# Starting the second layer pair's weight preparation earlier, behind other work and with three places

## The chip, the cores and the metric

The kernel runs on one core of a Trainium2 chip. The metric is the device time of one launch in microseconds (us), the median of several runs. Engines are TensorE (PE in the profile; PEld is its weight load), VectorE (DVE), ScalarE (ACT), GpSimd (POOL) and SyncE (SP), which issues all DMA transfers here.

## The reference

```python
# attention: 4 x 8 heads, 768 positions, head size 64, chunks of 32 with 16 keys to the left, 8 to the right, 8 memory keys
out[:, :, c_start:c_end] = softmax(q_c @ k_full.T / sqrt(D)) @ v_full
x = attn_out as (3072 tokens, 512)
# first layer pair ("moe"): w_in 512 x 2048, w_out 2048 x 512
h = x @ w_in
x = (h * clip(h + 3, 0, 6) / 6) @ w_out
# second layer pair ("moe2"), same shapes
h = x @ w_in
return maximum(0.01 * h, h) @ w_out
```

## The kernel before, in words

All products are made of fp32 values that are split into two fp32r parts, a high one and a low one; three products (high by high, low by high, high by low) stand for one. The tokens are cut into six blocks of 512 (`N`). The first layer pair works on units: unit f of block j makes 128 columns of the hidden layer (`hidden`, L602: 12 matmuls at L615, then `gate` at L627 on ACT, `times` at L630 on DVE, and the split `two_parts`, a cast on ACT and a subtraction), and `output` (L642) multiplies them by 128 rows of the second weight into four PSUM banks (12 matmuls at L662). TensorE takes hidden of unit i, then output of unit i - 1. Blocks 0 and 1 (`TWICE` = 2) are done in halves: block 0 units 0 to 7, block 1 units 0 to 7, block 0 units 8 to 15, block 1 units 8 to 15. So their output sums leave the banks twice: the first halves go through the `ys` tiles to `half` in DRAM, and at the end of the second half `y_out` (L681) reads them back (L699), adds the bank (`plus`, L696) and stores the sum to `spill` (L703). The other blocks' sums are copied once (`take`, L689) and stored to `spill`.

The second layer pair takes blocks in pairs of 1024 tokens and uses seven products instead of eight on 2 x 2 blocks. Its operands of activations come from `x_pair` (L715, with `x_quarter`, L725): loads from `spill`, subtractions on DVE, and splits. Its weights are prepared once, in the course of the first pair, by `prepare` (L788), 16 times, for w_in (kept as `kepti`) and w_out (`kepto`) in turn. One preparation:

- two calls of `decode` (L327): each loads 512 KB (L332) into one of the 33 `w` tiles, 32 of which hold the first pair's weights, takes an absolute value on ACT (L335) into one of two `wm` tiles and does four operations on DVE (L338 to L350). The loads come `after=splits[-2:]`, the last two splits of the first pair's weights; `gate=chain` puts ACT's operation behind the preparation before.
- four sums and differences of quarters (`form`, L804; L805) in place in the `wm` tiles, and seven times `parts_of` (L807): a high part (cast on ACT) and a low part (DVE) into one of the four `ys` tiles, which `keep` (L782) stores to DRAM (L784). The `ys` tile is free again when the store has landed.

`left` (L827) loads the kept parts back later (L835).

The order of all instructions comes from a planner, `schedule` (L83). It runs the tasks through a model of the engines at build time: each engine has a heap of ready tasks, and takes the one with the lowest key. Keys are positions in TensorE's sequence of products, in which a unit of the first pair takes 6; `progress` counts how far TensorE has come. A task is put in a heap when what it depends on is done and its key is at most `progress + AHEAD` (60). A task that needs new tiles (`allocs`) waits until there is a place (`blocked`, L108). The engines then execute the planned order strictly, each its own queue, with semaphore waits. The first pair takes keys 0 to 576; the preparations have keys 200 + 21 k (`PREPARE`, `EVERY`), their loads 30 less; `x_pair` for the first pair of blocks has keys 510 and 528; a gate's key is its unit's position less 12.

Of the kernel before, what the change touches and what calls it, by code (L numbers as in the profile page):

```python
# [9 lines left out]
F32 = mybir.dt.float32  # L10
# [31 lines left out]
LEFT_OF = {1: "a11", 2: "a12", 3: "s4", 4: "a22", 5: "s1", 6: "s2", 7: "s3"}  # L42
ORDER = FIRST + THEN
RING, OPS = 6, 6
PREPARE, EVERY = 200, 21
T1_IN = ("wm", "wm", "st", "st", "r", "r")
RIGHT_OF = {1: "b11", 2: "b21", 3: "b22", 4: "t4", 5: "t1", 6: "t2", 7: "t3"}

# [2 lines left out]
class Task:  # L51


    def __init__(self, fn, opts, key, after=(), allocs=(), uses=(), moe=False, issues=1):
        self.fn, self.opts, self.key, self.moe, self.issues = fn, opts, key, moe, issues
        self.allocs, self.next, self.left, self.ready = allocs, [], 0, 0.0
        self.bufs = list(allocs) + list(uses)
        self.taken = False
        for b in self.bufs:
            b.users += 1  # L60
        for t in after:
            t.next.append(self)
            self.left += 1


class Buf:


    def __init__(self, tag):
        self.tag, self.users, self.t = tag, 0, None  # L70


QUEUED = 6000.0
# [3 lines left out]
OTHER = 20  # L77
# [5 lines left out]
def schedule(tasks, places):  # L83
# [15 lines left out]
    def offer(task):  # L99
        nonlocal n  # L100
        n += 1
        if task.key > progress + AHEAD:
            heapq.heappush(future, (task.key, n, task))
            return
        for i, e in enumerate(task.opts):
            heapq.heappush(heaps[e], (task.key + (OTHER if i else 0), n, task))

    def blocked(task):  # L108
        for b in task.allocs:
            if len(live[b.tag]) >= places[b.tag]:  # L110
                return b.tag
        return None

# [94 lines left out]
def tile_attn_moe_moe2(ctx: ExitStack, tc: tile.TileContext, raw, w1i, w1o, w2i, w2o, out):  # L208
# [115 lines left out]

    wbuf, wtask = {}, {}

    def decode(src, f, key, early=None, after=(), place="wm", gate=()):  # L327

        t, m = Buf("w"), Buf(place)

        def load(e):
            nc.sync.dma_start(out=make(t, ([128, 512, 2], U32)).rearrange("p w s -> p (w s)"), in_=src[f])  # L332

        def absolute(e):
            nc.scalar.activation(out=make(m, ([128, 512], F32)), in_=t.t[:, :, 1].bitcast(F32), func=AF.Abs)  # L335

        def clamp(e):
            engine(e).tensor_scalar(out=m.t, in0=m.t, scalar1=W_MOST, scalar2=W_LEAST, op0=ALU.min, op1=ALU.max)  # L338

# [12 lines left out]
        k = add(load, {"SP": dma(524288)}, key - 30 if early is None else early, after=after, allocs=[t])  # L352
        k = add(absolute, {"ACT": act(512)}, key, after=[k, *gate], allocs=[m], uses=[t])
        k = add(clamp, {"DVE": dve2(512)}, key + 0.1, after=[k], uses=[m])
        k = add(bits, {"DVE": dve2(512)}, key + 0.2, after=[k], uses=[m])
        k = add(sign, {"DVE": dve(512)}, key + 0.3, after=[k], uses=[m, t])
        k = add(low, {"DVE": dve(512)}, key + 0.4, after=[k], uses=[m, t])
        return m, k

    def split_w(which, f, m, k, key):  # L360
# [219 lines left out]
            to_x(jb + 1, t, pos_h["1", jb + 1, 0] - BLK + 4, 0, first, NU, src=st)  # L580


    gbuf, gtask, yend, ybuf, yhalf, firsts = {}, {}, {}, {}, {}, []
    last = [None]

    def product(fn, n, after, allocs=(), uses=(), count=4):
# [52 lines left out]
    def bank(b):  # L639
        return made(b)  # L640

    def output(lay, j, f, c0, n):  # L642
        t0 = blocks[j][0]

        halves = (KF // 2, KF) if j < TWICE else (KF,)
        begin = c0 == 0 and f in (0, *halves)
        end = f + 1 in halves
        if begin:
            ybuf[lay, j] = banks_of(False)
        banks = ybuf[lay, j]  # L650
        ys = banks
        g, w = gbuf[lay, j, f, c0], wbuf[lay + "o", f]
        ghi, glo = gtask[lay, j, f, c0]
        whi, wlo = wtask[lay + "o", f]
        order = [(d, p) for p in range(3) for d in range(KD)]
        if end:
            order.sort()

        def part(some):
            def fn(e):  # L660
                for d, p in some:
                    nc.tensor.matmul(  # L662
                        bank(banks[d])[:, c0:c0 + n], w.t[:, 1 if p == 1 else 0, d * 128:(d + 1) * 128], g.t[:, 1 if p == 2 else 0, :n],
                        start=(begin and p == 0), stop=(end and p == 2), skip_group_check=True,
                    )
            return fn

        ks = []
        for i in range(3):
            some = order[4 * i:4 * i + 4]  # L670
            need = [whi, wlo, ghi] if end or i else [whi, ghi]
            if end or i == 2:
                need.append(glo)

            ks.append(product(part(some), n, need, allocs=ys if begin and i == 0 else (), uses=[w, g] + ([] if begin and i == 0 else ys)))
        if end:
            yend[lay, j] = []
            for d in range(KD):
                y_out(lay, j, f, t0, N, d, banks[d], ks[(3 * d + 2) // 4], len(halves) > 1)

    def y_out(lay, j, f, t0, n, d, y, k, two):  # L681
        s = Buf("ys")
        key = pos_y[lay, j, f] - 12
        scale = 1.0 / 6.0
        dst = spill[d, :, t0:t0 + n]
        if two and f < KF - 1:
            dst = half[j, d]

        def take(e):  # L689
            if e == "ACT":  # L690
                nc.scalar.mul(make(s)[:, :n], bank(y)[:, :n], scale)
            else:
                nc.vector.tensor_scalar(out=make(s)[:, :n], in0=bank(y)[:, :n], scalar1=scale, scalar2=None, op0=ALU.mult)

        def plus(e):
            nc.vector.scalar_tensor_tensor(out=s.t, in0=bank(y), scalar=scale, in1=s.t, op0=ALU.mult, op1=ALU.add)  # L696

        if two and f == KF - 1:
            l = add(lambda e: nc.sync.dma_start(out=make(s), in_=half[j, d]), {"SP": dma(n * 512)}, key - 8, after=[yhalf[j, d], *firsts], allocs=[s])  # L699
            k = add(plus, {"DVE": dve(n)}, key, after=[k, l], uses=[s, y])  # L700
        else:
            k = add(take, {"DVE": dve(n)} if d % 2 and two else {"ACT": act(n, 50.0)}, key, after=[k], allocs=[s], uses=[y])
        k = add(lambda e: nc.sync.dma_start(out=dst, in_=s.t[:, :n]), {"SP": dma(n * 512)}, key, after=[k], uses=[s])  # L703
        yhalf[j, d] = k
        if two and f < KF - 1:
            firsts.append(k)
        yend[lay, j].append(k)
# [74 lines left out]
    def keep(which, slot, src, after, uses, key):  # L782
        def fn(e):
            nc.sync.dma_start(out=kept[which][slot // 2, :, slot % 2], in_=src().bitcast(F32))  # L784

        kdone[which, slot] = add(fn, {"SP": dma(262144, 330.0)}, key, after=after, uses=uses)

    def prepare(which, src, i, key):  # L788


        parts = [decode(src, 2 * i + c, key + 6 * c, after=splits[-2:], gate=chain) for c in range(2)]
        raws, l = [m for m, _ in parts], [k for _, k in parts]
        chain[:] = l
        key += 12
# [7 lines left out]
            return raws[c].t[:, o:o + 256]  # L802

        def form(out, x, y, op, after):  # L804
            return [add(lambda e: engine(e).tensor_tensor(out=part(out), in0=part(x), in1=part(y), op=op), {"DVE": dve(256)}, key, after=after, uses=raws)]  # L805

        def parts_of(n, after):  # L807
            t, b = Buf("ys"), raws[at[n][0]]
            hi = add(lambda e: copy(e, make(t, ([128, 2, 256], F32R))[:, 0], part(n)), {"ACT": act(256)}, key, after=after, allocs=[t], uses=[b])
            lo = add(lambda e: minus(e, t.t[:, 1], part(n), t.t[:, 0].bitcast(F32)), {"DVE": dve(256)}, key, after=[hi], uses=[b, t])  # L810
            q = [LEFT_OF[m] for m in ORDER].index(n)
            keep(which, 7 * i + q if which == "i" else KF // 2 * q + i, lambda: t.t, [hi, lo], [t], key + 2)
            return [hi, lo]
# [341 lines left out]
```

## Time and profile before

| | us |
|---|---|
| median of 3 runs (lowest, highest) | 1114.21 (1111.7, 1115.73) |
| the profiled execution | 1105.18 |
| its span, first to last instruction | 1103.4 |
| TensorE busy in the span | 1061.6 |
| VectorE busy | 707.5 |
| ScalarE busy | 532.0 |

Times in the trace are counted from the start of the span. "Busy" counts instructions in flight; matmuls overlap, so TensorE's busy time is not its peak. In a timeline, a row has the start, the time taken, the engine, the line, and the operation as output <- inputs with buffer numbers left out; in brackets stands the idle time before it and what released it. "SPq" is the queue of SyncE with the time that an issue took there.

### The profile page before, as it was taken

The page shows a single profiled execution, that of the slowest core. Times are in us where ns is not written, and L with a number is a line of the kernel's source. Part 1 is how long each engine was busy: PE and PEld are TensorE (multiplying, and loading weights), DVE is VectorE, ACT ScalarE, POOL GpSimd, SP SyncE. Part 2 cuts the span into 40 slices and gives each one's busy share as a digit, 9 for nine tenths or more (in the row PEclk, how much of TensorE's full clock was granted, in tenths as well). Part 3 has the DMA queues.
Part 4 walks back from the last instruction along what each step waited for, and adds up shares of the span by engine and source line. Part 5 has one row for each costly group of instructions (what it writes and reads, how often), then busy time and mean ns, then how long its engine had stood idle before and what let it go on. Part 6 is the DMA issues. An engine that isn't in the chain of part 4 may idle for free.

```text
span 1103.4 us, 19981 instructions
## 1 busy us (share of the span) xinstructions
PE 1061.6 (96%) x7488; PEld 872.8 (79%) x7488; DVE 707.5 (64%) x1230; ACT 532.0 (48%) x1297; POOL 114.2 (10%) x112
## 2 busy tenths in 40 slices
PE   4599999999999999999999899999999999999998
PEld 3487888888878788788887688888888888888887
DVE  4789982526666566466678435499466696366673
ACT  4657554525666555455455333375234464233532
POOL 1130000101223222212222200000000000000000
PEclk9999999999999999999999999999999999999999
DMA  8886414505566555365477346668765786766763
GB/s 198 246 221 203 172 65 113 156 22 182 173 179 199 159 175 191 124 188 170 139 239 254 106 143 224 236 219 323 256 220 211 266 294 248 249 221 226 260 217 115
DMA packets 105120, 215.22 MB, mean 195 GB/s; under 512 B 10816, under 2 KB 43584, under 8 KB 105024
## 3 DMA queue, kind: packets, MB, share of 16 engines
q1 hardware_dynamic: 105024, 213.95, 59.3%
q8 instruction: 59, 0.97, 0.4%
q14 instruction: 37, 0.30, 0.1%
HBM read 163.58 MB, written 50.33 MB: 194 GB/s over the span
## 4 chain that ended last, share of the span: by engine, by line
PE 77%; DVE 7%; DMA 7%; ACT 3%; SPq 2%; issue 2%; POOL 0%; ACTq 0%; DVEq 0%
PE y L662 17%; PE h L615 17%; PE y L997 12%; PE y L879 10%; PE h L997 6%; PE hx L879 6%; PE h L879 4%; PE hx L997 3%; DMA w<-in_raw 2%; DMA a<-in_raw 2%; DMA w<-in_w1o 2%; DVE ys L292 1%; PE at L493 1%; SPq L397 1%; DVE wm L346 1%
## 5 line engine op out<-in xcount | busy, mean ns | idle before, releaser
L662 PE MATMUL y<-g,w 128*128 128x512 f32 x1152 | 283.8, 393 | 8.1 <-ACT g L289 5.3
L662 PEld LDWEIGHTS y<-g,w 128*128 128x128 f32 x1152 | 216.2, 189 | 56.5 <-ACT g L289 6.6
L615 PE MATMUL h<-xh,w 128*128 128x512 f32 x768 | 196.3, 395 | 1.6 <-ACT xh L289 1.6
L615 PEld LDWEIGHTS h<-xh,w 128*128 128x128 f32 x768 | 143.7, 189 | 32.5 <-ACT xh L289 2.6
L630 DVE SCALAR_TENSOR_TENSOR r<-r,h 128x512 f32<-128x512 f32 x96 | 65.8, 685 | 106.8 <-ACT r L627 106.7
L292 POOL TENSOR_TENSOR g<-r,g 128x512 fp32r<-128x512 f32 x64 | 88.6, 1385 | 332.0 <-ACT g L289 315.3
L627 ACT ACTIVATE r<-h,three 128x512 f32<-128x512 f32 x96 | 66.5, 693 | 109.0 <-PE h L615 108.5
L292 DVE TENSOR_TENSOR w<-w 128x512 fp32r<-128x512 f32 (+1 forms) x162 | 105.5, 687 | 17.4 <-ACT w L289 16.5
L615 PE MATMUL h<-xl,w 128*128 128x512 f32 x384 | 104.1, 393 | 0.0
L854 ACT ACTIVATE w<-w 128x512 f32<-128x512 f32 x48 | 30.3, 632 | 132.1 <-DVE w L911 100.2
L997 PE MATMUL y<-w 128*128 128x512 f32 x384 | 90.0, 389 | 0.0
L289 ACT CAST g<-r 128x512 fp32r<-128x512 f32 x97 | 60.5, 624 | 58.2 <-DVE r L630 53.3
L615 PEld LDWEIGHTS h<-xl,w 128*128 128x128 f32 x384 | 72.3, 189 | 15.4
L997 PEld LDWEIGHTS y<-w 128*128 128x128 f32 x384 | 72.1, 188 | 15.0
L292 DVE TENSOR_TENSOR ys<-wm,ys 128x256 fp32r<-128x256 f32 x112 | 61.2, 568 | 20.4 <-ACT ys L289 20.2
L879 PE MATMUL y<-w 128*128 128x512 f32 x264 | 61.8, 389 | 0.0
L289 ACT CAST g<-w 128x512 fp32r<-128x512 f32 x50 | 31.0, 622 | 63.8 <-PE y L997 34.3
L289 ACT CAST w<-w 128x512 fp32r<-128x512 f32 x102 | 58.3, 618 | 6.2 <-DVE w L292 4.5
L879 PEld LDWEIGHTS y<-w 128*128 128x128 f32 x264 | 49.6, 188 | 10.3
L335 ACT ACTIVATE wm<-w 128x512 f32<-128x512 f32 x56 | 37.6, 673 | 33.3 <-DVE ys L292 9.2
L289 ACT CAST ys<-wm 128x256 fp32r<-128x256 f32 x112 | 41.8, 410 | 23.5 <-DVE wm L350 14.6
L292 DVE TENSOR_TENSOR g<-w,g 128x512 fp32r<-128x512 f32 x50 | 34.0, 689 | 28.7 <-ACT g L289 28.5
(160 smaller groups left out, 1515.8 us busy)
## 6 DMA issues: line engine op xcount, KB each, us to landing
w<-kepti SPq DMA_DIRECT2D x84, 512.0 KB
w<-kepto SPq DMA_DIRECT2D x84, 512.0 KB
kepti<-ys SPq DMA_DIRECT2D x56, 256.0 KB
kepto<-ys SPq DMA_DIRECT2D x56, 256.0 KB
a<-in_raw SPq DMA_DIRECT2D x44, 224.0 KB
w<-in_w1i SPq DMA_DIRECT2D x16, 512.0 KB
w<-in_w1o SPq DMA_DIRECT2D x16, 512.0 KB
w<-in_w2i SPq DMA_DIRECT2D x16, 512.0 KB
```

The costliest lines, as they stand in the source:

```text
L289: nc.scalar.copy(out, in_) if e == "ACT" else engine(e).tensor_copy(out=out, in_=in_)
L292: engine(e).tensor_tensor(out=out, in0=a, in1=b, op=ALU.subtract)
L335: nc.scalar.activation(out=make(m, ([128, 512], F32)), in_=t.t[:, :, 1].bitcast(F32), func=AF.Abs)
L346: nc.vector.scalar_tensor_tensor(out=mu, in0=t.t[:, :, 1], scalar=0xC0000000, in1=mu, op0=ALU.bitwise_and, op1=ALU.bitwise_or)
L397: nc.sync.dma_start(out=qk[i].t[r], in_=of_raw(par, r, slice(0, QK))[i].rearrange("g d c -> d g c"))
L615: nc.tensor.matmul(h.t[:, :n], w.t[:, 1 if p == 1 else 0, k * 128:(k + 1) * 128], x[:, k, c0:c0 + n], start=(p == 0 and k == 0), stop=(p = ...
L627: nc.scalar.activation(out=make(r)[:, :n], in_=h.t[:, :n], func=AF.Relu, bias=three[:, 0:1], scale=1.0)
L630: nc.vector.scalar_tensor_tensor(out=r.t[:, :n], in0=r.t[:, :n], scalar=6.0, in1=h.t[:, :n], op0=ALU.min, op1=ALU.mult)
L662: nc.tensor.matmul(bank(banks[d])[:, c0:c0 + n], w.t[:, 1 if p == 1 else 0, d * 128:(d + 1) * 128], g.t[:, 1 if p == 2 else 0, :n], start= ...
L854: return add(lambda e: nc.scalar.activation(out=at(), in_=at(), func=AF.Prelu, alpha=0.01), {"ACT": act(N)}, key, after=[after], uses=uses)
L879: nc.tensor.matmul(bank(to), t.t[:, o, l, kt * 128:(kt + 1) * 128].bitcast(F32R), operand(p, name, 1 if q == 2 else 0, kt).bitcast(F32R), ...
L997: nc.tensor.matmul(bank(to[d]), w.t[:, o, 1 if q == 1 else 0, d * 128:(d + 1) * 128].bitcast(F32R), g.t[:, 1 if q == 2 else 0], start=(fre ...
```

## The change

Preparation k has the key 112 + 22 k instead of 200 + 21 k. All its tasks but the loads get `late=60`: this is added to their key for the rank in an engine's heap, but not for the moment from which they may be taken. Its parts may take a `ys` tile only while that leaves at most three of the four in use (`Buf("ys", 3)`). A task that needs several tiles of a kind at once (the four banks of an output, or two) waits until there is room for all of them.

The reload of a half sum now begins with a one-column copy on ACT that takes the `ys` tile and waits for the last product of output unit f - 3 (`ylast`); the DMA follows it. The copies of the first half sums, of which two in four ran on DVE, run on ACT.

```diff
-PREPARE, EVERY = 200, 21
+PREPARE, EVERY, LATE = 112, 22, 60
...
 class Buf:
-    def __init__(self, tag):
-        self.tag, self.users, self.t = tag, 0, None
+    def __init__(self, tag, most=99):
+        self.tag, self.most, self.users, self.t = tag, most, 0, None
...
         for i, e in enumerate(task.opts):
-            heapq.heappush(heaps[e], (task.key + (OTHER if i else 0), n, task))
+            heapq.heappush(heaps[e], (task.key + task.late + (OTHER if i else 0), n, task))
...
     def blocked(task):
+        tags = [b.tag for b in task.allocs]
         for b in task.allocs:
-            if len(live[b.tag]) >= places[b.tag]:
+            if len(live[b.tag]) + tags.count(b.tag) > min(places[b.tag], b.most):
                 return b.tag
...
+        ylast[j, f] = ks[-1]
         if end:
...
         def take(e):
-            if e == "ACT":
-                nc.scalar.mul(make(s)[:, :n], bank(y)[:, :n], scale)
-            else:
-                nc.vector.tensor_scalar(out=make(s)[:, :n], in0=bank(y)[:, :n], scalar1=scale, scalar2=None, op0=ALU.mult)
+            nc.scalar.mul(make(s)[:, :n], bank(y)[:, :n], scale)
...
         if two and f == KF - 1:
-            l = add(lambda e: nc.sync.dma_start(out=make(s), in_=half[j, d]), {"SP": dma(n * 512)}, key - 8, after=[yhalf[j, d], *firsts], allocs=[s])
+            l = add(lambda e: nc.scalar.copy(make(s)[:, :1], three), {"ACT": act(1)}, key - 8, after=[yhalf[j, d], *firsts, ylast[j, f - 3]], allocs=[s])
+            l = add(lambda e: nc.sync.dma_start(out=s.t, in_=half[j, d]), {"SP": dma(n * 512)}, key - 8, after=[l], uses=[s])
             k = add(plus, {"DVE": dve(n)}, key, after=[k, l], uses=[s, y])
         else:
-            k = add(take, {"DVE": dve(n)} if d % 2 and two else {"ACT": act(n, 50.0)}, key, after=[k], allocs=[s], uses=[y])
+            k = add(take, {"ACT": act(n, 50.0)}, key, after=[k], allocs=[s], uses=[y])
...
-        kdone[which, slot] = add(fn, {"SP": dma(262144, 330.0)}, key, after=after, uses=uses)
+        kdone[which, slot] = add(fn, {"SP": dma(262144, 330.0)}, key, after=after, uses=uses, late=LATE)
...
-            t, b = Buf("ys"), raws[at[n][0]]
+            t, b = Buf("ys", 3), raws[at[n][0]]
```

The other lines pass `late=LATE` to the operations of `decode`, `form` and `parts_of`.

## Rows read from the trace of the kernel before

**Rows 1.** The page, part 1: busy us, share of the span, instructions.

```profile
PE 1061.6 (96%) x7488; PEld 872.8 (79%) x7488; DVE 707.5 (64%) x1230; ACT 532.0 (48%) x1297; POOL 114.2 (10%) x112
```

**Rows 2.** TensorE's waits: releaser, us in total, times, longest us.

```profile
PE y L662 <- ACT g L289: 5.3, 2, 4.6
...
PE y L662 <- ACT ys L691: 2.8, 2, 2.3
```

**Rows 3.** Windows by stage: stretch, length, busy (instructions) per engine, clock, DMA share, GB/s.

```profile
160.00:255.00 95.00, 95.00 (x873) 78.11 (x873) 37.48 (x65) 38.40 (x118) 4.38 (x4) 1.00 0.35 95
255.00:560.00 305.00, 301.05 (x2678) 246.09 (x2677) 193.11 (x349) 169.62 (x499) 73.59 (x54) 1.00 0.55 172
560.00:618.00 58.00, 52.65 (x223) 42.30 (x222) 50.25 (x90) 30.08 (x61) 14.25 (x10) 0.97 0.72 239
636.00:1103.00 467.00, 463.53 (x2046) 383.48 (x2044) 293.03 (x459) 193.13 (x334) 1.29 (x1) 1.00 0.66 232
```

**Rows 4.** Timeline from 605 to 618 us.

```profile
605.93 0.68 ACT L627 ACTIVATE r<-h,three 128x512 f32<-128x512 f32 x1
...
607.85 1.07 PE L615 MATMUL h<-xl,w 128*128 128x512 f32 x4
...
612.19 0.68 DVE L630 SCALAR_TENSOR_TENSOR r<-r,h 128x512 f32<-128x512 f32 x1
...
612.90 0.62 ACT L289 CAST g<-r 128x512 fp32r<-128x512 f32 x1 [2.15 <-DVE r L630]
...
613.57 4.50 PE L662 MATMUL y<-g,w 128*128 128x512 f32 x12 [4.65 <-ACT g L289]
```

**Rows 5.** The chain of work that ended last: start, us, twelve output matmuls.

```profile
626.25 2.72 PE y L662 x12
```

**Rows 6.** VectorE's groups from 560 to 620 us, of preparation: busy us, mean ns.

```profile
L292 DVE TENSOR_TENSOR ys<-wm,ys 128x256 fp32r<-128x256 f32 x26 | 16.0, 641 | 2.0 <-ACT ys L289 2.0
L805 DVE TENSOR_TENSOR wm<-wm 128x256 f32<-128x256 f32 x15 | 7.3, 490 | 0.1
```

**Rows 7.** Timeline of SyncE's queue: reloads, first load, spills, first and last stores.

```profile
168.12 1.77 SPq L699 DMA_DIRECT2D ys<-half  x4
169.93 0.43 SPq L332 DMA_DIRECT2D w<-in_w2i  x1
170.40 11.75 SPq L397 DMA_DIRECT2D a<-in_raw  x4
...
206.93 0.35 SPq L703 DMA_DIRECT2D spill<-ys  x1
...
257.15 1.32 SPq L703 DMA_DIRECT2D spill<-ys  x3
259.38 0.32 SPq L784 DMA_DIRECT2D kepti<-ys  x1
...
608.74 8.66 SPq L784 DMA_DIRECT2D kepto<-ys  x7
```

**Rows 8.** Timeline of ACT, one cycle of preparation, 505 to 527 us.

```profile
505.23 1.02 ACT L289 CAST ys<-wm 128x256 fp32r<-128x256 f32 x3 [2.68 <-DVE wm L350]
...
511.67 0.44 ACT L289 CAST ys<-wm 128x256 fp32r<-128x256 f32 x1
513.73 0.72 ACT L335 ACTIVATE wm<-w 128x512 f32<-128x512 f32 x1
...
523.41 0.67 ACT L335 ACTIVATE wm<-w 128x512 f32<-128x512 f32 x1 [0.35 <-DMA w<-in_w2o]
526.63 1.01 ACT L289 CAST ys<-wm 128x256 fp32r<-128x256 f32 x3
```

**Rows 9.** Timeline around 157 us: last split of the first pair's weights.

```profile
157.10 0.62 ACT L289 CAST w<-wm 128x512 fp32r<-128x512 f32 x1
```

**Rows 10.** ACT's prices: ns min/median/max of copies; group of accumulator reads, us, ns.

```profile
L691 ACT ACTIVATE ys<-y x20: 580/598/628, 112.2 to 648.1; 128x512 f32<-128x512 f32 x20
...
L462 ACT ACTIVATION_READ_ACCUMULATOR a<-at,mx 128x1 f32 x132 | 30.2, 229 | 0.0
```

More of the change, by code (lines that the diff above doesn't have):

```diff
@@ L51, with __init__ @@
 class Task:
-    def __init__(self, fn, opts, key, after=(), allocs=(), uses=(), moe=False, issues=1):
+    def __init__(self, fn, opts, key, after=(), allocs=(), uses=(), moe=False, issues=1, late=0):
+        self.late = late
         self.fn, self.opts, self.key, self.moe, self.issues = fn, opts, key, moe, issues
@@ L325, in tile_attn_moe_moe2, with decode @@
     wbuf, wtask = {}, {}
-    def decode(src, f, key, early=None, after=(), place="wm", gate=()):
+    def decode(src, f, key, early=None, after=(), place="wm", gate=(), late=0):
         t, m = Buf("w"), Buf(place)
@@ L352, in decode @@
         k = add(load, {"SP": dma(524288)}, key - 30 if early is None else early, after=after, allocs=[t])
[L353 to L357, printed above, removed]
+        k = add(absolute, {"ACT": act(512)}, key, after=[k, *gate], allocs=[m], uses=[t], late=late)
+        k = add(clamp, {"DVE": dve2(512)}, key + 0.1, after=[k], uses=[m], late=late)
+        k = add(bits, {"DVE": dve2(512)}, key + 0.2, after=[k], uses=[m], late=late)
+        k = add(sign, {"DVE": dve(512)}, key + 0.3, after=[k], uses=[m, t], late=late)
+        k = add(low, {"DVE": dve(512)}, key + 0.4, after=[k], uses=[m, t], late=late)
         return m, k
@@ L580, in unit @@
             to_x(jb + 1, t, pos_h["1", jb + 1, 0] - BLK + 4, 0, first, NU, src=st)
-    gbuf, gtask, yend, ybuf, yhalf, firsts = {}, {}, {}, {}, {}, []
+    gbuf, gtask, yend, ybuf, yhalf, ylast, firsts = {}, {}, {}, {}, {}, {}, []
     last = [None]
@@ L784, in fn @@
             nc.sync.dma_start(out=kept[which][slot // 2, :, slot % 2], in_=src().bitcast(F32))
-        kdone[which, slot] = add(fn, {"SP": dma(262144, 330.0)}, key, after=after, uses=uses)
+        kdone[which, slot] = add(fn, {"SP": dma(262144, 330.0)}, key, after=after, uses=uses, late=LATE)
     def prepare(which, src, i, key):
-        parts = [decode(src, 2 * i + c, key + 6 * c, after=splits[-2:], gate=chain) for c in range(2)]
+        parts = [decode(src, 2 * i + c, key + 6 * c, after=splits[-2:], gate=chain, late=LATE) for c in range(2)]
         raws, l = [m for m, _ in parts], [k for _, k in parts]
@@ L804, in form @@
         def form(out, x, y, op, after):
-            return [add(lambda e: engine(e).tensor_tensor(out=part(out), in0=part(x), in1=part(y), op=op), {"DVE": dve(256)}, key, after=after, uses=raws)]
+            return [add(lambda e: engine(e).tensor_tensor(out=part(out), in0=part(x), in1=part(y), op=op), {"DVE": dve(256)}, key, after=after, uses=raws, late=LATE)]
         def parts_of(n, after):
-            t, b = Buf("ys"), raws[at[n][0]]
-            hi = add(lambda e: copy(e, make(t, ([128, 2, 256], F32R))[:, 0], part(n)), {"ACT": act(256)}, key, after=after, allocs=[t], uses=[b])
-            lo = add(lambda e: minus(e, t.t[:, 1], part(n), t.t[:, 0].bitcast(F32)), {"DVE": dve(256)}, key, after=[hi], uses=[b, t])
+            t, b = Buf("ys", 3), raws[at[n][0]]
+            hi = add(lambda e: copy(e, make(t, ([128, 2, 256], F32R))[:, 0], part(n)), {"ACT": act(256)}, key, after=after, allocs=[t], uses=[b], late=LATE)
+            lo = add(lambda e: minus(e, t.t[:, 1], part(n), t.t[:, 0].bitcast(F32)), {"DVE": dve(256)}, key, after=[hi], uses=[b, t], late=LATE)
             q = [LEFT_OF[m] for m in ORDER].index(n)
```

## The prediction

> **What bounds the kernel now.** I began with the busy shares on the page: TensorE has an instruction in flight for 1061.6 of 1103.4 us, VectorE for 707.5 [rows 1]. So the question is where TensorE stands idle, 41.8 us in all, and which of that the change can reach. The windows by stage answer the first half: from 160 to 255 us it loses nothing, from 255 to 560 us 3.95, from 560 to 618 us 58.0 - 52.65 = 5.35 us, and from 636 us to the end 3.5 us of 467 [rows 3]. The remaining 29 us lie nearly all before 160 us, ahead of any preparation. The list of TensorE's waits then names two that stand in the middle of the span: 5.3 us for a gate's cast (ACT g), 4.6 us of it in one place, and 2.8 us for output copies (ACT ys) [rows 2].
>
> The timeline around 605 to 618 us shows the one large wait. A gate (L627) ends at 606.61, but VectorE comes to its product (L630) only at 612.19; the cast follows at 612.90 and the output matmuls at 613.57, while the last hidden matmul had ended at 608.92 [rows 4]. So TensorE stands for 4.65 us behind VectorE's queue. The twelve matmuls after it take 4.50 us, against 2.72 us for the same twelve soon afterwards [rows 4, 5]: another 1.78 us, and the granted clock of the stretch is 0.97 instead of 1.00 [rows 3], so some of them ran at the lower of its two levels, 1.2 GHz, after TensorE had stood. Earlier in the same tail there is a wait of 0.66 us of the same kind (the rest of the 5.3 us). The tail costs 5.3 + 1.8 = 7.1 us.
>
> What fills VectorE there? Of its 50.25 us in that stretch, the preparation's splits and forms alone (L292 on ys, L805) take 16.0 + 7.3 = 23.3 us [rows 3, 6], beside the bit work on the same weights and the first operands of the second pair. Preparation and x_pair fall on each other.
>
> **Why it is late.** The preparation is a chain, and not held up by keys. The row of stores shows its first store at 259.38 and its last seven from 608.74 [rows 7], 15 cycles of 23.3 us. One cycle reads as follows: first part cast at 505.23, the fifth at 511.67 (the first to get a place back, 6.4 us later), the next preparation's first half decoded from 513.73, its second half from 523.41, first part cast at 526.63 [rows 8]. It starts late because all four ys places are full: the reloads of block 0's half sums are issued at 168.12 though its spills leave only at 206.93, and block 1's hold the places until its spills at 257.15 [rows 7]. The first weight load was out at 169.93 [rows 7].
>
> **The change part by part.**
> *Start.* The key of 112 is not what decides: the loads still wait for the last two splits of the first pair, whose cast is at 157.10 [rows 9]. So the first load can go at about 158 instead of 169.93. What decides is that the reloads now wait for the output of unit f - 3. From the end of that unit to the next needed bank there are five groups of twelve matmuls and then the first bank's three: 5 x 2.72 + 0.68 = 14.3 us [rows 5]. The places are then held for some 20 us at each of the two block ends instead of from 168 to 257 us nearly without a break. Following a cycle by hand with the durations of rows 8: preparation 0 forms its parts from about 176, preparation 1 from about 212 (behind block 0's reloads), preparation 2 from 231 with a break at block 1's end, and preparation 3 begins decoding at about 259. Before, preparation 0 stood there: two preparations and some 7 us, 2 x 23.3 + 7 = 54 us of lead.
>
> *Cap of three.* Bounds: nothing, or one more turn of a place, 6.4 us a preparation [rows 8]. The next decode needs the raw half that the fourth and fifth parts use last. With four places the fifth part is the first of the second round; with three it is the second of that round, so it comes only a fraction of a microsecond later, and only the seventh part slips by a whole round, which the next half's load covers. I take 0.8 us, near the lower end: 13 x 0.8 = 10 us of the lead. Perfetto Trace Analysis in the Trainium skill, under "Identifying the Most-Contended Engine", says that gaps that repeat can mean that there are too few buffers; taking a place away would then lengthen every cycle by the upper bound. By that rule 13 x 6.4 = 83 us would eat all of the lead and the sum would have no gain in it; no run here shows it yet. By the rows the sum keeps 54 - 10 = 44 us of lead. How it would go without that is a rival below.
>
> *Rank.* The 60 is mostly taken back by the earlier keys: the last preparation's key was 200 + 15 x 21 = 515 and is 112 + 15 x 22 + 60 = 502. It matters while preparation is ahead, where its instructions now stand behind gates. Cost: VectorE is busy 37.48 of 95 us in the stretch that receives them [rows 3], so I take no slowing there. SyncE's part moves too, 32 loads and 112 stores, none added; the DMA engines are busy 0.35 of the stretch that receives the first of them [rows 3], so again nothing. GpSimd does none of the preparation.
>
> *End.* The last cycles of before are shorter than the mean, since places of w that the first pair frees let their loads run ahead; cycles that end sooner have less of that. So I count on two thirds of the 44 us and expect the last store near 617 - 30 = 587 us. Two preparations leave the stretch 560 to 618, half of the four that it holds now, and none is left beside the second half of x_pair after 594 us. The two groups of rows 6 alone are 23.3 / 50.25 = 46% of VectorE's work in the stretch, so the product, 5.6 us late now, comes some 3 us or more earlier, and with the bit work gone too, early enough. Gain 7.1 us; I leave 0.5 us for x_pair alone.
>
> *Reloads.* Eight one-column ACT copies are added. No row shows one; the nearest are the one-column accumulator reads, 229 ns, and a full copy, 598 ns [rows 10]. I take 0.23 us each: 1.8 us of ACT, hidden, since ACT is busy 38.40 of 95 us there [rows 3]. They wait for TensorE and for a place in ACT's queue, and gates stand behind them. A reload needs a place (up to 6.4 us), the copy, and a landing (with 6 us as a bound from the place's whole turn): 12.6 us against 14.3, plus 2.72 us of hidden matmuls before a bank is missed, 4.4 us of slack. Bounds 0 and a late reload (rival); I take 0.5 us.
>
> *Copies.* At the ends of the first two half blocks, ACT takes four instead of two, 2 x 0.60 us more [rows 10]; banks become ready 0.68 us apart and the next output is 2.72 us away, so nothing; without that cover 1.2 us each. The 2.8 us that later copies cost [rows 2] come from stores that hold ys places. The kept place serves one copy of four, the others still wait for stores: I take 0, with bounds of a gain of 2.8 and a loss of 2.8 us. The stricter count of banks changes the planner's idea of when TensorE may start, not what the hardware waits for: 0, with 0.5 us either way hidden in the same slack. For denser queues from 160 to 560 us I put 0.5 us.
>
> Sum: 7.1 - 0.5 - 0.5 - 0.5 = 5.6 us off. The profiled execution took 1105.18 us, 1.8 us beyond its span; it would come to 1099.6. The median of the runs shown is 1114.21, above all that the profiled execution shows, so I take the ratio: 1114.21 x 1099.6 / 1105.18 = 1108.6 us. A difference of 0.3% (3.3 us) is about what a measurement can tell from none.
>
> **Rivals.**
> (a) *The copies' wait goes as well*, because one place is always theirs: 7.1 + 2.8 = 9.9 us, 1104.2 us. For it: the wait is named by its ys place; against: four copies, one place. Chance 0.08.
> (b) *Preparation ends no earlier.* The cap or the rank lengthens each cycle by 3.5 us or more, 13 x 3.5 = 45 us, and the tail collides as now: 1114 us. For it: the cycle is a chain of place turns [rows 8]; against: the fifth part is in the second round with three places too. This is also the case that the earlier start does nothing. Chance 0.19.
> (c) *Slower: a reload behind a blocked queue.* SyncE issues in order, and one group of attention loads held it for 11.75 us at 170.40 [rows 7]. If such a group stands ahead of a late reload, the sums come 11.75 - 4.4 = 7.4 us late, TensorE stands with full banks and restarts slowly (1.8 us): 9.2 us, net 9.2 - 5.6 = 3.6 us lost, 1117.8 us; at both block ends 1127. It outweighs the gain from a hold of 4.4 + 5.6 - 1.8 = 8.2 us on. For it: the last attention units go through the same stretch and queue; against: the planner gives the reloads a better key than stores and most loads there. Chance 0.15.
>
> **How the numbers follow.** The likeliest case has 0.58, with its own range of 1106 to 1111. Faster by over 0.3%: it and (a), less the weak end, 0.62. Within 0.3%: most of (b) and that weak end, 0.22. Slower: (c) and a little of (b), 0.16. The range reaches from below (a) to the single late reload: 1103.5 to 1117.5.
>
> **What would show it.** Right: first store to kept weights near 180 instead of 259 us, last near 590; no wait over 1 us for a gate's cast between 560 and 620 us, and a granted clock of 1.00 there; reloads some 14 us ahead of the sums. The cap is right if a cycle is under 25 us. Wrong: last store after 605 us (b); a wait of TensorE near 205 or 251 us whose releaser is a sum at L696 or its reload (c); or new waits for gates behind ACT's one-column copies, which I have put at nothing.

## The result, and the profile after

The changed kernel takes 1093.52 us (median of 6 runs, 1091.86 to 1094.38), the kernel before 1112.57 us in as many (1108.5 to 1115.73). The ratio is 0.9829, with a 95% interval of 0.9807 to 0.985: 19 us off, where the prediction had 5.6 us off and a range whose lower end was 1103.5. The direction was right and the size wrong by more than a factor of three.

The profiled execution of after took 1094.38 us with a span of 1092.6 us. Its page, part 1, against [rows 1]:

```profile
PE 1055.7 (97%) x7488; PEld 870.8 (80%) x7488; DVE 707.5 (65%) x1227; ACT 533.8 (49%) x1309; POOL 113.5 (10%) x111
```

The work is the same: 7488 matmuls, and VectorE busy for 707.5 us as before. The windows of after by stage, with the columns of [rows 3]:

```profile
160.00:255.00 95.00, 95.00 (x874) 78.22 (x873) 53.07 (x102) 46.38 (x136) 1.52 (x3) 1.00 0.50 159
255.00:560.00 305.00, 304.76 (x2705) 250.97 (x2704) 198.83 (x350) 171.98 (x509) 76.77 (x56) 1.00 0.56 175
560.00:618.00 58.00, 58.00 (x257) 48.05 (x256) 33.81 (x57) 24.93 (x48) 13.95 (x11) 1.00 0.47 159
636.00:1092.00 456.00, 452.72 (x1998) 374.71 (x1996) 290.25 (x455) 190.55 (x330) 0.00 (x0) 1.00 0.67 238
```

From 160 to 618 us TensorE now stands for 0.24 us in all. VectorE's 50.25 us in the tail have become 33.81, and the stretch from 160 to 255 us has taken on 53.07 - 37.48 = 15.6 us. SyncE's queue of after shows what moved, against [rows 7]:

```profile
159.79 0.37 SPq L334 DMA_DIRECT2D w<-in_w2i  x1
...
181.48 1.35 SPq L785 DMA_DIRECT2D kepti<-ys  x3
...
192.32 1.79 SPq L700 DMA_DIRECT2D ys<-half  x4
208.93 1.92 SPq L704 DMA_DIRECT2D spill<-ys  x4
...
221.84 8.11 SPq L785 DMA_DIRECT2D kepto<-ys  x6
...
239.14 1.74 SPq L700 DMA_DIRECT2D ys<-half  x4
...
254.81 0.32 SPq L704 DMA_DIRECT2D spill<-ys  x1
...
265.45 4.78 SPq L785 DMA_DIRECT2D kepti<-ys  x4
...
590.11 0.32 SPq L785 DMA_DIRECT2D kepto<-ys  x1
```

The first store to the kept weights comes at 181.48 instead of 259.38, the last at 590.11 instead of 617. The reloads go out at 192.32 and 239.14, some 16 us ahead of the spills that follow at 208.93 and 254.81.

To see where the time went, the matmuls of the first pair were counted in groups of twelve (hidden and output in turn, attention left out), and the starts of the same groups compared. The table is worked out from the matmul records of each trace. Groups 72 to 168 hold the ends of blocks 2, 3 and 4 (groups 96, 128, 160); groups 168 to 192 are the tail, the last of them being the first twelve matmuls of the second pair. From group 192 to the start of the last matmul each of these traces takes 456.73 us, and from 32 to 72 each takes 120.2 to 120.3.

```
execution                      span      72-168    168-192
before, first profile          1103.4    294.26    73.11
before, second (e1)            1110.3    295.67    78.14
before, third (e9)             1105.2    293.47    74.90
after                          1092.6    288.23    65.28
e2  after, old reloads         1094.6    288.61    69.24
e3  after, old keys            1091.4    288.68    65.78
e4  after, no cap              1098.3    294.45    65.55
e5  before, no GpSimd in tail  1099.5    293.75    67.15
e6  before, cap                1100.6    288.22    72.09
e7  before, reloads            1094.4    288.00    69.63
e8  before, rank               1100.9    296.57    66.35
e10 after, no rank             1092.1    289.77    66.19
e11 after, small parts undone  1089.4    288.05    65.28
e12 before, cap and reloads    1094.5    288.75    68.25
```

Twenty-four groups of 2.72 us make 65.28 us: after has nothing left to lose in the tail. Against the first profile of before it won 7.83 us there and 6.03 us in the stretch of the block ends. It began 3.0 us later: group 32 starts at 157.86 us in after and at 154.83 in before, which gives the 10.8 us between the spans. This start differs between executions, from 154.8 (e11) to 159.1 us (e6) in these traces; what sets it stays open. The granted clock does not sort it: from 40 to 60 us it was 0.50 in after, at the lower level of 1.2 GHz, 0.53 in e11 and 1.00 in e6. That leaves the question why the runs differ by 19.

### The profile page after: what moved, and what is told of

Its sections match the earlier page's. It is cut to its first block, busy times and chain, and to the rows that moved or that the text cites. A ratio compares the mean times of both kernels' runs of the same rounds, so it can differ in the third digit from the quotient of the medians.

```text
span 1092.6 us, 19983 instructions
## 1 busy us (share of the span) xinstructions
PE 1055.7 (97%) x7488; PEld 870.8 (80%) x7488; DVE 707.5 (65%) x1227; ACT 533.8 (49%) x1309; POOL 113.5 (10%) x111
## 4 chain that ended last, share of the span: by engine, by line
PE 91%; DMA 4%; SPq 2%; DVE 2%; ACT 1%; issue 1%; ACTq 0%; DVEq 0%
PE y L664 23%; PE h L617 23%; PE y L998 12%; PE y L880 10%; PE h L998 6%; PE hx L880 6%; PE h L880 4%; PE hx L998 3%; DMA w<-in_w1i 2%; PE at L495 1%; DMA w<-in_raw 1%; PE at L434 1%; SPq L399 1%; PE at L484 1%; SPq L410 0%
## 5 line engine op out<-in xcount | busy, mean ns | idle before, releaser
L664 PE MATMUL y<-g,w 128*128 128x512 f32 x1152 | 280.7, 391 | 0.0
L632 DVE SCALAR_TENSOR_TENSOR r<-r,h 128x512 f32<-128x512 f32 x96 | 65.7, 684 | 92.2 <-ACT r L629 91.6
L294 DVE TENSOR_TENSOR ys<-wm,ys 128x256 fp32r<-128x256 f32 x112 | 63.4, 593 | 23.1 <-ACT ys L291 23.0
```

Source lines behind the costliest of these rows:

```text
L294: engine(e).tensor_tensor(out=out, in0=a, in1=b, op=ALU.subtract)
L632: nc.vector.scalar_tensor_tensor(out=r.t[:, :n], in0=r.t[:, :n], scalar=6.0, in1=h.t[:, :n], op0=ALU.min, op1=ALU.mult)
L664: nc.tensor.matmul(bank(banks[d])[:, c0:c0 + n], w.t[:, 1 if p == 1 else 0, d * 128:(d + 1) * 128], g.t[:, 1 if p == 2 else 0, :n], start= ...
```

## The experiments

**e1, the kernel before once more.** No edit.

> The kernel before, unchanged, for a second profiled execution. The first profile of before (1105.2 us) lies below every timed run of before (1108.5 to 1115.7), and aligned unit by unit it explains 13.8 us of the gain from 160 us on, of about 19. Theory A (the collisions of preparation with gates and copies cost more in most executions than in the profiled one): this profile takes some 1112 us and TensorE loses 16 to 20 us between 255 and 640 us, where the first profile lost 9.3 us of idle time and 1.8 us of slow clock. Theory B (the rest lies ahead of the preparation, in the start): the losses from 255 to 640 us are again 11 us and the 7 us more lie before 160 us.

1110.2 us median, ratio 1.0008 (0.9987 to 1.0029); the profiled execution took 1112.07. TensorE's waits behind 110 us, and the timeline of its tail:

```profile
PE y L662 <- POOL g L292: 7.1, 1, 7.1
PE y L662 <- ACT ys L691: 2.8, 2, 2.3
PE y L662 <- ACT g L289: 2.0, 2, 1.3
```

```profile
605.13 2.11 PE L662 MATMUL y<-g,w 128*128 128x512 f32 x8
605.15 9.10 POOL L292 TENSOR_TENSOR g<-r,g 128x512 fp32r<-128x512 f32 x1 [5.56 <-PE h L615]
605.21 0.42 DVE L342 TENSOR_SCALAR wm<-wm 128x512 uint32<-128x512 uint32 x1
...
613.04 0.68 DVE L630 SCALAR_TENSOR_TENSOR r<-r,h 128x512 f32<-128x512 f32 x1
613.64 1.16 DVE L292 TENSOR_TENSOR w<-a,w 128x512 fp32r<-128x512 f32 x1
614.31 2.07 PE L662 MATMUL y<-g,w 128*128 128x512 f32 x4 [7.07 <-POOL g L292]
616.18 3.52 PE L615 MATMUL h<-xh,w 128*128 128x512 f32 x8
```

The releaser is another than in [rows 2] and [rows 4]. The subtraction for the gate's low part, which GpSimd does for the later blocks, took 9.10 us, and all that time VectorE went through its queue without a break. The last four matmuls of the output group waited for it for 7.07 us, and the matmuls after it ran slowly. The same two instructions in the first profile of before:

```profile
603.19 1.30 POOL L292 TENSOR_TENSOR g<-r,g 128x512 fp32r<-128x512 f32 x1 [5.56 <-PE h L615]
603.25 1.52 DVE L342 TENSOR_SCALAR wm<-wm 128x512 uint32<-128x512 uint32 x1
```

There GpSimd was quick and VectorE's instruction took 1.52 us instead of 0.42: each engine can hold up the other, and which one it is differs between executions, though GpSimd starts 0.06 us before that instruction in both. The Trainium skill (SBUF — State Buffer, "Who interferes with whom") says that GpSimd reads through a port pair that VectorE shares, and that the order of issue decides who is blocked. The rows agree that one of the two holds up the other; the ports themselves no row shows. They differ in how long: the page has the block last for an instruction, here GpSimd was held up through nearly 8 us of VectorE's queue. Nor do the rows bear out that the order decides: by the starts in the profile it was the same in both executions, and the winner was not. Theory A holds: against after, this execution loses 20.3 us from group 72 on, the first profile 13.9. The 6.4 us between them lie in the tail (78.14 against 73.11) and a little at the block ends (295.67 against 294.26). The timed runs point the same way: of 15 runs of before beside e1 to e4, seven took 1105.3 to 1107.6 us, eight 1111.2 to 1115.7, and none lay between.

**e2, after with the old reloads.**

```diff
-            l = add(lambda e: nc.scalar.copy(make(s)[:, :1], three), {"ACT": act(1)}, key - 8, after=[yhalf[j, d], *firsts, ylast[j, f - 3]], allocs=[s])
-            l = add(lambda e: nc.sync.dma_start(out=s.t, in_=half[j, d]), {"SP": dma(n * 512)}, key - 8, after=[l], uses=[s])
+            l = add(lambda e: nc.sync.dma_start(out=make(s), in_=half[j, d]), {"SP": dma(n * 512)}, key - 8, after=[yhalf[j, d], *firsts], allocs=[s])
```

> The changed kernel with the reloads of the half sums issued as before (no one-column copy, no wait for unit f - 3). Theory A (full ys places set the start of preparation): the first store to kept weights comes again near 255 to 260 us, the last after 605 us, TensorE stands again 4 us or more for a gate's cast in the tail, 1100 to 1112 us. Theory B (the earlier key sets the start): first store before 200 us, last near 590 us, no such wait, 1093 us as the changed kernel.

1097.94 us, ratio 0.9898 (0.986 to 0.9936). The stores to kept weights run from 263.1 to 626.7 us, so full places do hold up the start, with the early key and all. TensorE's waits behind 110 us:

```profile
PE y L664 <- POOL g L294: 3.0, 2, 2.7
PE h L617 <- ACT xh L291: 1.6, 1, 1.6
PE y L664 <- ACT g L291: 0.6, 1, 0.6
```

The tail loses 4.0 us (69.24), with GpSimd's subtraction held up for 4.75 us. Theory A was right on the start, but wrong on the releaser, and its 1100 to 1112 us were too many, since it had the whole tail come back: preparation that ends at 627 us costs 4 us here, and 8 to 13 us in before, where it ends at 617 to 625. When it ends is not the whole story.

**e3, after with the old keys.**

```diff
-PREPARE, EVERY, LATE = 112, 22, 60
+PREPARE, EVERY, LATE = 200, 21, 60
```

> The changed kernel with the keys of before, 200 + 21 k, and all the rest of the change (rank 60 behind, cap of three, new reloads). Theory A (the places decide, since a key may be taken 60 ahead): first store to kept weights by 200 us, last by 600 us, 1093 to 1096 us. Theory B (the keys decide): first store after 210 us, last store after 605 us, and a wait for a gate's cast in the tail comes back, 1100 us or more.

1093.18 us, ratio 0.9859 (0.9826 to 0.9892). First store at 218.3 and last at 608.1 us: both as theory B had it, so where places are free, the key does set the start. But no wait comes back, with 65.78 us in the tail, and the time is that of after, as in theory A. The earlier key, which names the change, buys nothing that these runs can tell.

**e4, after without the cap.**

```diff
-            t, b = Buf("ys", 3), raws[at[n][0]]
+            t, b = Buf("ys"), raws[at[n][0]]
```

> The changed kernel without the cap: preparation may fill all four ys places. Theory A (the cap hardly touches the pace, and the place that it keeps is what took away the copies' wait): cycles within 1 us of the capped ones, last store within 5 us of 590 us, and 2 to 6 us of waits for output copies come back at the ends of blocks 2 to 4, 1096 to 1099 us. Theory B (the wait of the copies went with the rank): no wait for copies, 1093 us.

1100.07 us, ratio 0.9917 (0.9885 to 0.9948). First store at 180.7, last at 586.2 us, the tail clean (65.55), but 6.2 us lost at the block ends, nearly all of it behind block 3 (5.9 us at group 130). The end of block 3 in its timeline:

```profile
450.25 0.40 ACT L291 CAST ys<-wm 128x256 fp32r<-128x256 f32 x1
450.55 0.60 ACT L693 ACTIVATE ys<-y 128x512 f32<-128x512 f32 x1
...
451.64 0.59 ACT L693 ACTIVATE ys<-y 128x512 f32<-128x512 f32 x1
...
452.13 0.40 ACT L291 CAST ys<-wm 128x256 fp32r<-128x256 f32 x1
...
457.07 0.59 ACT L693 ACTIVATE ys<-y 128x512 f32<-128x512 f32 x1
...
460.39 0.62 ACT L693 ACTIVATE ys<-y 128x512 f32<-128x512 f32 x1
...
461.06 3.79 PE L664 MATMUL y<-g,w 128*128 128x512 f32 x9 [2.84 <-ACT ys L693]
```

Parts of preparation took ys places at 450.25 and 452.13; with the first two copies that makes four, and in the planned order the third and fourth copy come only after stores have landed. The same end in after:

```profile
451.30 0.60 ACT L693 ACTIVATE ys<-y 128x512 f32<-128x512 f32 x1
452.29 1.59 ACT L693 ACTIVATE ys<-y 128x512 f32<-128x512 f32 x3
```

So the kept place took this wait away (theory A; the time lies 1.1 us above its range), and it does not make preparation slower: cycles of 23.8 us in after (from the fourth preparation's first store at 290.96 to the fourteenth's at 528.87) and of 24.9 us over the same preparations here.

**e5, before with GpSimd kept out of the last block.**

```diff
-        two_parts(lay, j, f, r, k, key, {"DVE": 600.0} if j < TWICE else {"POOL": pool(n), "DVE": dve(n)})
+        two_parts(lay, j, f, r, k, key, {"DVE": 600.0} if j < TWICE or j == len(blocks) - 1 else {"POOL": pool(n), "DVE": dve(n)})
```

> The kernel before, with the low part of every gate of the last block (units 80 to 95) subtracted on VectorE; GpSimd may take none of them. In two profiles of before one subtraction on GpSimd took 1.30 us and 9.10 us in the tail, with VectorE busy without a break beside the long one. Theory A (GpSimd's subtraction is held up while VectorE runs without a break, in some executions, and this makes the 7 us by which executions of before differ): the timed runs lie closer together, under 4 us from lowest to highest where before has 10, with a median of 1102 to 1107 us. Theory B (the spread has another source): the same spread and 1110 us or more.

1101.42 us, ratio 0.9913 (0.9891 to 0.9934), runs from 1099.24 to 1105.19. VectorE has 16 subtractions more to do in the last block, and the tail falls from 73 to 78 us to 67.15. The median came just under theory A's range of 1102 to 1107 us. Its other half failed: six runs spread over 6.0 us, the 11 runs of before beside them over 6.4. So GpSimd in the tail costs time, but that it makes the spread of before is not shown; the start, which differs by some 4 us between traces, is another source. The copies' waits are left (3.0 us).

**e6, before with the cap alone** (`Buf` takes `most=99` as in the change).

```diff
-            if len(live[b.tag]) >= places[b.tag]:
+            if len(live[b.tag]) >= min(places[b.tag], b.most):
...
-            t, b = Buf("ys"), raws[at[n][0]]
+            t, b = Buf("ys", 3), raws[at[n][0]]
```

> The kernel before with the cap alone: parts of preparation may take a ys tile only while at most three are in use. Theory A (the cap keeps a place for the output copies and spreads the preparation's bursts): no wait of TensorE for output copies over 0.5 us (2.8 us before), the tail's wait is halved though the last store to kept weights is not earlier than 615 us, 1098 to 1104 us. Theory B (the cap serves the copies alone): copies' waits gone, the tail as before, 1105 to 1108 us.

1100.76 us, ratio 0.9894 (0.9865 to 0.9923). The block ends are clean (288.22 against 293.5 to 295.7). The tail still loses 6.8 us, with the last seven stores from 622.3 to 632.7 us; its waits, and its window from 600 to 625 us:

```profile
PE y L662 <- POOL g L292: 2.7, 1, 2.7
...
PE y L662 <- ACT g L289: 0.6, 1, 0.6
```

```profile
600.00:625.00 25.00, 21.68 (x82) 17.04 (x81) 20.36 (x40) 11.97 (x24) 7.78 (x3) 0.86 0.26 95
```

The wait was more than halved against e1, but half of the loss is the lower clock behind it (0.86 granted). So theory A is right on the copies, and on the time by its range; that the tail is relieved by the cap rests on this one execution.

**e7, before with the new reloads alone**, which is e2's edit the other way round, and `ylast`.

```diff
+        ylast[j, f] = ks[-1]
...
-            l = add(lambda e: nc.sync.dma_start(out=make(s), in_=half[j, d]), {"SP": dma(n * 512)}, key - 8, after=[yhalf[j, d], *firsts], allocs=[s])
+            l = add(lambda e: nc.scalar.copy(make(s)[:, :1], three), {"ACT": act(1)}, key - 8, after=[yhalf[j, d], *firsts, ylast[j, f - 3]], allocs=[s])
+            l = add(lambda e: nc.sync.dma_start(out=s.t, in_=half[j, d]), {"SP": dma(n * 512)}, key - 8, after=[l], uses=[s])
```

> The kernel before with the new reloads alone (one-column copy, wait for unit f - 3). Theory A (full places set the start, and the lead removes the tail's collision): first store to kept weights before 225 us, last before 605 us, no wait for a gate over 1 us from 560 to 640 us, but the copies' waits stay at 2 to 6 us, 1098 to 1103 us. Theory B (the lead alone does not help, the rank does): tail wait of 4 us or more stays, 1106 to 1112 us.

1097.89 us, ratio 0.9879 (0.9856 to 0.9901). First store at 218.1, last at 597.4 us. Both theories were missed in detail: a wait of 2.6 us for GpSimd stays in the tail (69.63), and the copies' waits, which nothing in this edit guards, are gone (288.00). Here the parts of preparation fell behind the copies (first casts after them at 361.75 and 453.50 us); e4 has the same reloads and 6.2 us of such waits. So without the cap it is chance, as far as the runs show, where the parts fall in the planned order.

**e8, before with the rank alone** (every task of preparation gets `late=LATE`, as in the change).

```diff
-PREPARE, EVERY = 200, 21
+PREPARE, EVERY, LATE = 200, 21, 60
...
-            heapq.heappush(heaps[e], (task.key + (OTHER if i else 0), n, task))
+            heapq.heappush(heaps[e], (task.key + task.late + (OTHER if i else 0), n, task))
```

> The kernel before with the rank alone: the tasks of preparation but the loads rank 60 behind, at the old keys 200 + 21 k; no cap, reloads, copies and count as before. Theory A (gates ahead of preparation in VectorE's queue remove the tail's wait even when preparation ends late): last store to kept weights after 615 us, but no wait for a gate over 1 us from 560 to 640 us, 1098 to 1104 us. Theory B (the rank does little, since the dense queue of VectorE holds GpSimd up all the same): a wait of 4 us or more there, 1105 to 1112 us.

1104.06 us, ratio 0.9932 (0.9907 to 0.9957). Preparation ends last of all here, with stores to 640.8 us, and the tail is nearly clean: 66.35 us. The block ends are the worst of all (296.57). Its waits:

```profile
PE y L664 <- ACT ys L694: 3.9, 3, 2.3
...
PE y L664 <- POOL g L294: 0.7, 1, 0.7
PE y L664 <- ACT g L291: 0.6, 2, 0.3
```

Theory A holds on the waits, and the median lies just above its range: once gates stand ahead of preparation in VectorE's queue, a late preparation need not cost anything in the tail.

**e9, the kernel before a third time.** No edit.

> The kernel before, unchanged, a third profiled execution. Theory A (one subtraction on GpSimd in the tail is either quick or held up, and this sorts the executions of before): if it takes under 1108 us, no subtraction on GpSimd is over 3 us from 560 to 640 us and the units 168 to 184 take under 53 us; if it takes over 1109 us, one is over 6 us and these units take over 55 us. Theory B: the length of the subtraction and the time do not go together.

1106.96 us, a single execution. The tail takes 74.90 us. GpSimd was quick again:

```profile
603.65 1.30 POOL L292 TENSOR_TENSOR g<-r,g 128x512 fp32r<-128x512 f32 x1 [5.57 <-PE h L615]
603.70 1.52 DVE L342 TENSOR_SCALAR wm<-wm 128x512 uint32<-128x512 uint32 x1
...
614.03 5.49 PE L662 MATMUL y<-g,w 128*128 128x512 f32 x12 [4.67 <-ACT g L289]
```

The three executions that were profiled agree with theory A: 1105.18 and 1106.96 us with a subtraction of 1.30 us, 1112.07 us with one of 9.10; three are few. Over the groups 168 to 184, which the expectation's bounds of 53 and 55 us are for, the first profile takes 51.35, e1 56.38 and e9 53.14 us: the last misses its bound by 0.14 us, and after takes 43.52.

**e10, after without the rank.**

```diff
-PREPARE, EVERY, LATE = 112, 22, 60
+PREPARE, EVERY, LATE = 112, 22, 0
```

> The changed kernel with the rank taken out (keys 112 + 22 k, LATE = 0), cap, reloads, copies and count kept. Theory A (cap and reloads are enough; the rank adds little to them): last store to kept weights before 600 us, no wait for a gate over 1 us from 560 to 640 us, 1092 to 1096 us. Theory B (the rank carries several us even with the lead): waits for gates or copies of 3 us or more come back between 160 and 640 us, 1097 us or more.

1094.19 us, ratio 0.9836 (0.9816 to 0.9857). Theory A, but for the last store, at 602.9 us and not before 600: with cap and reloads the rank adds nothing that can be told. The tail takes 66.19 us, with one subtraction of 3.82 us on GpSimd that TensorE waited 0.6 us for.

**e11, after with the small parts undone**: first half sums copied by VectorE and ACT in turn, places counted one by one.

```diff
-            if len(live[b.tag]) + tags.count(b.tag) > min(places[b.tag], b.most):
+            if len(live[b.tag]) >= min(places[b.tag], b.most):
...
-            k = add(take, {"ACT": act(n, 50.0)}, key, after=[k], allocs=[s], uses=[y])
+            k = add(take, {"DVE": dve(n)} if d % 2 and two else {"ACT": act(n, 50.0)}, key, after=[k], allocs=[s], uses=[y])
```

> The changed kernel with its two small parts undone: the copies of the first half sums again run two on VectorE and two on ACT, and the planner counts places as before. Theory A (neither bears on the time): 1092 to 1096 us and no wait over 1 us from 160 to 640 us. Theory B (the stricter count gives the planner a true picture of the banks at block ends): waits of 2 us or more at the ends of blocks, 1096 us or more.

1091.54 us, ratio 0.9815 (0.9797 to 0.9833). Neither part bears on the time, as in theory A, though the median is 0.5 us under its range; the interval overlaps that of after (0.9807 to 0.985), so it can't be called faster than after. No wait of TensorE is listed behind 110 us at all.

**e12, before with cap and reloads**, the edits of e6 and e7 together.

> The kernel before with two parts of the change alone, the cap of three and the new reloads; keys 200 + 21 k, no rank, copies and count as before. Theory A (these two carry the whole gain): 1092 to 1096 us, no wait of TensorE over 1 us from 160 to 640 us, no subtraction on GpSimd over 4 us. Theory B (the earlier key or the rank is needed beside them): a wait of 2 us or more in the tail, 1097 us or more.

1095.71 us, ratio 0.9863 (0.9829 to 0.9897). Most of the gain, not all of it in this execution: the tail loses 3.0 us (68.25). Its waits:

```profile
PE y L662 <- ACT g L289: 1.8, 1, 1.8
PE y L662 <- POOL g L292: 1.0, 2, 0.6
```

The time is in theory A's range, the waits are in neither's. Whether the last 2 us come from the rank or the keys isn't settled: the kernel after keeps them without the keys (e3) and without the rank (e10), so one of the two seems enough. The intervals of e12 and after overlap, so the 2 us may also be none.

## Why the prediction was wrong

Counted from group 72 on, where the traces part, the change is worth 13.86 us on the execution that the prediction read, and 20.3 on e1. The sum had 5.6. So it was 8.3 us short on its own execution, and the base took away 6.4 more.

**One step that failed is the sum's base.** "The median of the runs shown is 1114.21, above all that the profiled execution shows, so I take the ratio": the prediction scaled its 1099.6 us by the ratio of 1114.21 to 1105.18, as if the 9 us between them were spread over the kernel. They were not. The three runs that were shown all lay above the profiled execution, by 6.5 us or more; the profile had caught a good execution of a tail that can go two ways. In e1 the tail cost 78.14 - 65.28 = 12.9 us, in e9 9.6, in the profile that was read 7.8. What the change removes is the tail's whole loss, in whichever way it falls out. A term of 7.1 us for the tail was close for the execution that was read (7.83), and too small for e1 and e9. A small part of it was misread: its 1.78 us set a timeline row of twelve matmuls against a step of the chain; a timeline row of twelve undisturbed ones takes 2.88 us, which leaves 1.62.

**The other, and the larger, is the copies.** "The kept place serves one copy of four, the others still wait for stores: I take 0, with bounds of a gain of 2.8 and a loss of 2.8 us." The stretch of the block ends gained 6.0 us, 7.4 against e1. Of the 6.0, 4.1 us lie behind the copies: 1.28 us at the end of block 2 (groups 97 to 105) and 2.81 at that of block 3 (group 130). The reasoning on places was wrong: banks become ready 0.68 us apart, and with at most three places in use by the time of the first copy, preparation is locked out while the copies take the rest (e4 against after). The size was too small as well: 2.8 us is the matmuls' idle time [rows 2], and TensorE ran slowly after it (group 130 took 5.53 us, 2.25 of them idle, for 2.72 in after). Rival (a) had this mechanism at 2.8 us, and a chance of 0.08. The other 1.9 us are a term that the sum lacked: they lie up to group 96 and at group 136, where TensorE in before waits 0.7 and 0.5 us for attention's operands from GpSimd and VectorE. Why these waits went is open. The costs in the sum, 0.5 us each for x_pair, the late reload and denser queues, did not show: the tail takes no more than its 24 undisturbed groups, and TensorE stands for 0.24 us in all from 160 to 560 us.

**What was right.** Full places hold up the start of preparation: with the old reloads the first store comes at 259 to 267 us, with the new key too (e2: 263). That the key "is not what decides" was only half right: with the new reloads it comes at 218 us with the old keys (e3, e7, e12) and at 179 to 181 with the new ones, so 41 us of the shift come from the reloads and 37 from the key. Nor did the tail need the early end that the text counted on: it is clean in e3, where the last store comes at 608 us, and nearly so in e8, at 641. The first store came at 181, where "near 180" was predicted, the last at 590 for 587 to 590; the cap left the cycle at 23.8 us, under the 25 that the text set and the 24.9 without it (e4), so rival (b) did not come. Nor did the rule on too few buffers in Perfetto Trace Analysis of the Trainium skill (it stands there under "Optimization Strategy") decide here: taking a place away made the cycle no longer, and without the cap (e4) the kernel loses 6 us. The lead was smaller than worked out: the third preparation's stores began at 265.45 instead of from 231, so after leads there by about two preparations less 6 us, 41 us instead of 54, and by 27 us at the last store. Rival (c) did not come: no wait of TensorE near 209 or 256 us, and the one-column copies took 0.186 us each for the 0.23 taken. Their row in ACT's timeline of after:

```profile
191.19 0.47 ACT L699 COPY ys<-three 128x1 f32<-128x1 f32 x4
```

**What the rivals lacked.** The text named VectorE's queue as the cause of the tail's wait. True for the gate's product, but the same dense queue has a second victim, GpSimd's subtraction, which is what TensorE waited for longest in the tails of e1, e2, e6 and e7. The rows of before could have shown it: VectorE's 1.52 us for an instruction that takes 0.42 elsewhere, beside a GpSimd instruction, was in the same timeline as [rows 4].

**The parts of the change.** Each of three parts gains alone on before: cap 11 us, reloads 14, rank 8 (ratios 0.9894, 0.9879, 0.9932). They overlap, since tail and copies can be lost only once: all together gain 19. The cap can't be left out of the rest (e4: 6.5 us lost), the reloads neither (e2: 4.4 us); rank, keys and small parts can, each by itself (e10, e3, e11). These gains are of whole plans, though: every edit goes through the planner and moves other instructions too, and each has one profiled execution. How much of a gain is the edit's own, and how much a luckier order (e7 lost its copies' waits with nothing to guard against them), the runs don't part.

## What to carry to other kernels

Where a profiled execution lies at the edge of the timed runs, the difference is a finding and not a scale factor: profile the kernel again, and look for instructions whose duration differs between the two. For a kernel whose order is fixed ahead, align equal pieces of the bounding engine's work between traces; that gives the loss of each stage, where lists of waits give only what stood idle in plain sight. When background work shares few buffers with work that the bounding engine waits for, keep a buffer out of its reach and don't let a prefetch hold them all: here each of these gained over 10 us alone (e6, e7), and the earlier key nothing that can be told beside them (e3).

## What the runs showed of the hardware

A subtraction of 128 x 512 values on GpSimd, 1.30 us in most places, took up to 9.10 us beside a VectorE that ran without a break. In all six runs where such a one took over 3.5 us, it ended 1.2 us after the start of VectorE's next gate product (`times`, L630 or L632), which alone of the instructions there reads a PSUM bank; the instruction behind the product then took nearly 0.5 us longer than usual. Worked out from the traces, in us:

```
run  starts  took  product starts  ends after that
e1   605.15  9.10  613.04          1.21
e2   603.25  4.75  606.80          1.21
e6   606.41  4.76  609.96          1.21
e7   586.32  5.16  590.27          1.20
e8   587.80  4.76  591.34          1.22
e10  585.42  3.82  588.02          1.22
```

In after one that took 3.29 us ended 1.15 us after VectorE had run out of work, and e4 has the same with 2.83. So what was held up got through at a gate product or at a pause, as far as these rows show; why, no run tests. In the first profile and in e9, at the same place in the same program as in e1, VectorE was held up instead, 1.52 us for 0.42. These three executions took 1105.18, 1106.96 and 1112.07 us; the tail makes 5.0 and 3.2 us of the last one's distance to the other two.
